# Sharing the setup of a short convolution among three engines, and reordering the mode mix behind it

## The chip, the cores and the metric

The kernel runs on one core of a Trainium2 chip. The core has a matrix engine (TensorE, PE in the rows), a vector engine (VectorE, DVE), an activation engine (ScalarE, ACT), GpSimd (POOL), and SyncE (SP). POOL issues all loads here, because they cast from float32 to bfloat16 on the way, and SP issues all stores. The metric is the time of one execution on the device, in microseconds (us).

## The reference

The input x has 8 batches of 3264 rows of 192 channels. First each row becomes a weighted sum of itself and the six rows ahead of it, with seven weights per group of 24 channels (8 groups). Then the 64 lowest Fourier modes along the rows are mixed by a complex 192x192 matrix each, and transformed back, and a dense layer with a relu is added.

```python
w = softmax(weight, axis=-1)                    # (8 groups, 7 taps)
x = einsum('hk,bskhg->bshg', w, windows_of_7(x)) # causal, zeros ahead of row 0
X = rfft(x, axis=1)[:, :64]
Yr = Xr @ w_r - Xi @ w_i                        # for each mode, 192x192
Yi = Xr @ w_i + Xi @ w_r
u = x + irfft(Yr + 1j * Yi, n=3264)
out = u + maximum(u @ w_ch, 0)
```

## The kernel before

The rows of a batch are cut into 27 windows of 122 rows. A window is loaded with the six rows ahead of it as 128 partitions, and all of x stays in SBUF as `x_all`. The work runs in three stages, in an order that is written out in the code: each engine works through its own queue in that order.

**Stage one: setup, convolution and Fourier transform.** The convolution of a group of channels is one matmul with a band matrix `cband[:, h, :]` (128x128, the seven taps on seven diagonals). VectorE builds the eight bands: for each tap, `copy_predicated` (L163) writes the tap's weight where the mask `maskk` of that diagonal is set, four groups at a time. VectorE also prepares the angles for the Fourier matrix `fst` (`kprod`, `turns`, L167 to L173), and ScalarE turns them into sines and cosines (`make_f`, L176 to L178). A batch is three units (10, 8 and 9 windows), 24 units in all. For a unit, `conv_unit` makes two halves of four matmuls each into one of two PSUM buffers, and ScalarE copies each half back over `x_all` (L233). `dft_unit` then multiplies the unit's windows with `fst` (L284); it follows the convolution by 5 units at the start and by 1 at the end (`lag`). After a batch's third unit VectorE copies the sums out (`xs`, L288), PE sorts them by mode (L296), and VectorE writes them to `xt` (L298).

**Stage two: the mode mix.** It has 16 groups of four modes. In each group PE multiplies `xt` with the modes' weights (`yp`, L349), ScalarE copies the product (`ymix`), PE transposes it (`et`), and VectorE writes `yeT`. Weights lie in tiles `wt` of two modes with six buffers (`MG = 2`, L205): a group's two tiles are loaded anew as soon as its matmuls are through, for use three groups later. Between these steps the 24 units of x are transposed into `cT` for the last stage (`t_unit`): VectorE first copies the upper 64 channels together (`make_tail`, L240 to L243, two buffers), PE transposes some 14 blocks into two PSUM tiles `tp` (L271), and VectorE copies each out (L273). Two units stand in each of groups 0 to 7, one in each later group. `g_part` transposes `fst` in groups 8 to 11.

**Stage three: the output.** For each pair of batches and windows PE sums the inverse transform and the dense layer in PSUM (`group_z`), ScalarE applies the relu (L409), PE adds the plain sum (`group_y`), VectorE adds x (L425), and SP stores.

```python
for _ in range(2 if g < 8 else 1):
    if tq and g < NG4 - 1:
        t_unit(*tq.pop(0))
if gq and g >= 8:
    g_part(gq.pop(0))
```

Of the kernel before, what the change touches and what calls it, by code (L numbers as in the profile page):

```python
# [9 lines left out]
ALU = mybir.AluOpType  # L10
# [8 lines left out]
def kernel(  # L19
# [24 lines left out]
    GW = NWIN * WIN + 6  # L44
    MG = 2
    NGRP = MODES // MG
# [18 lines left out]
    def load_unit(b, u):  # L65
# [10 lines left out]
        else:  # L76
# [25 lines left out]
                   allow_small_or_imprecise_dtypes=True)  # L102
    load_unit(0, 0)
    load_unit(0, 1)
    maskk = sp.tile([P, KK, P], BF16, tag="maskk")
# [6 lines left out]
    for u in range(3):  # L112
        load_unit(1, u)
    nc.gpsimd.memset(ident[:], 0.0)
    nc.gpsimd.affine_select(out=ident[:], in_=ident[:], compare_op=ALU.not_equal, fill=1.0,
                            base=0, pattern=[[-1, P]], channel_multiplier=1)

# [5 lines left out]
    for b in range(2, B):  # L123
        for u in range(3):
# [9 lines left out]
                            in1=midx[:, :].unsqueeze(1).to_broadcast([P, NWIN, MODES]),  # L134
                            op=ALU.mult)
    wmax = sp.tile([P, H], F32, tag="wmax")
    nc.vector.reduce_max(out=wmax[:], in_=wraw[:], axis=AX.X)
# [4 lines left out]
    nc.scalar.activation(out=wexp[:], in_=wsub[:], func=ACT.Exp)  # L142
    nc.vector.memset(cband[:], 0.0)
    wsum = sp.tile([P, H], F32, tag="wsum")
# [9 lines left out]


    wps = pxx.tile([P, 512], F32, tag="xp", name="wps")
    wsb = wps[:, 0:H * KK].rearrange("p (h k) -> p h k", h=H)
    nc.vector.tensor_tensor(out=wsb, in0=wexp[:],
                            in1=wrec[:, :].unsqueeze(2).to_broadcast([P, H, KK]), op=ALU.mult)
    for half in range(2):  # L160
        hs = slice(4 * half, 4 * half + 4)
        for k in range(KK):
            nc.vector.copy_predicated(  # L163
                out=cband[:, hs, :],
                mask=maskk[:, k, :].bitcast(mybir.dt.uint16).unsqueeze(1).to_broadcast([P, 4, P]),
                data=wsb[:, hs, k:k + 1].to_broadcast([P, 4, P]))
    nc.vector.tensor_scalar(out=turns[:], in0=kprod[:], scalar1=1.0 / S, scalar2=MAGIC,  # L167
                            op0=ALU.mult, op1=ALU.add)
    nc.vector.tensor_scalar(out=turns[:], in0=turns[:], scalar1=-MAGIC, scalar2=float(S),
                            op0=ALU.add, op1=ALU.mult)  # L170
    nc.vector.tensor_tensor(out=kprod[:], in0=kprod[:], in1=turns[:], op=ALU.subtract)
    nc.vector.tensor_scalar(out=kprod[:], in0=kprod[:], scalar1=-float(S) / 2, scalar2=float(S) / 2,
                            op0=ALU.max, op1=ALU.min)  # L173

    def make_f():
        nc.scalar.activation(out=turns[:], in_=kprod[:], func=ACT.Abs)  # L176
        nc.scalar.activation(out=fst[:, :, 1:2 * MODES:2], in_=kprod[:], func=ACT.Sin, scale=-TWOPI / S)
        nc.scalar.activation(out=fst[:, :, 0:2 * MODES:2], in_=turns[:], func=ACT.Sin, scale=-TWOPI / S,  # L178
                             bias=halfpi[:, 0:1])
# [24 lines left out]

    wp = early_stack.enter_context(tc.tile_pool(name="wts", bufs=6, side="right"))  # L205
    wtiles = {}
# [7 lines left out]

    for g in range(6):
        load_weights(g)
    workp = early_stack.enter_context(tc.tile_pool(name="work", bufs=2, side="right"))

    def conv_unit(b, u):
        w0, n = UNITS[u]  # L220
        if u == 0 and b > 0:
            nc.vector.memset(x_all[0:OV, b, 0, :], 0.0)
        for half in range(2):
# [8 lines left out]
            srcv = cp[0:WIN, :, 0:GRP * n].rearrange("p j (w e) -> p j w e", w=n)  # L232
            nc.scalar.copy(out=dst, in_=srcv)  # L233

# [28 lines left out]

    def t_unit(b, u):
        s0, n = USLOTS[u]
        h1 = (n + 1) // 2
        tl = make_tail(b, u)
# [37 lines left out]
    for i, (b, u) in enumerate(units):  # L305
        conv_unit(b, u)
        if i == 3:
            make_f()
            setup_stack.close()
# [30 lines left out]
    NG4 = MODES // 4  # L340
    tq = [(b, u) for b in range(B) for u in range(3)]
    gq = list(range((NWIN + 7) // 8))
    for g in range(NG4):
        yp = pconv.tile([P, 512], F32, tag="cv", name="yp")
        for j in range(3):
            for pos in range(4):
# [4 lines left out]
                                 start=(j == 0), stop=(j == 2), tile_position=(0, 32 * pos))  # L351
        for i in range(4 // MG):
            n = 6 + (4 // MG) * g + i
            if n < NGRP:
                load_weights(n)
# [12 lines left out]
        if g == NG4 - 2:  # L368
            while tq:
                t_unit(*tq.pop(0))  # L370
    early_stack.close()
# [132 lines left out]
```

## Time and profile before

| what | value |
|---|---|
| median of 3 runs | 230.06 us (228.36 to 232.61) |
| profiled execution, its own time | 230.81 us |
| span of its instructions | 229.1 us |
| PE busy | 167.1 us, 73% |
| DVE busy | 116.4 us, 51% |
| ACT busy | 101.4 us, 44% |
| POOL busy | 70.6 us, 31% |
| read from and written to HBM | 40.31 MB and 20.05 MB |

Busy times are sums over the whole span. The three stages have different limits, so a stage is read by itself: what it waits for, and what ends that wait. A row of the kind "start, length, engine, line" is one instruction or several merged ones, and the bracket at its end says how long the engine had been idle and who released it.

### The profile page before, as it was taken

What the parts mean: (1) busy time and instruction counts of PE and PEld (TensorE: products, weight loads), DVE (VectorE), ACT (ScalarE), POOL (GpSimd) and SP (SyncE); (2) the same over time, 40 slices, a digit from 0 to 9 for tenths busy, and PEclk for the clock granted to TensorE, in tenths of its full rate; (3) what the DMA queues carried; (4) which work ended last, traced back from release to release, by engine and by line L of the source; (5) the groups of instructions that cost most, each with busy time, mean ns of one, the idle gap of its engine ahead of it and who ended that gap; (6) DMA issues with size and microseconds to landing.
All of it is one profiled execution on the core that took longest, in us unless ns stands there. A gap on an engine that the chain in (4) does not pass through costs nothing.

```text
span 229.1 us, 4342 instructions
## 1 busy us (share of the span) xinstructions
PE 167.1 (73%) x1699; PEld 131.8 (58%) x1699; DVE 116.4 (51%) x211; ACT 101.4 (44%) x132; POOL 70.6 (31%) x121
## 2 busy tenths in 40 slices
PE   0037349989988786768869679999899899989300
PEld 0014248777877564547647458778677677767200
DVE  7897001111111577776654615677676566666510
ACT  2017978778687010100431126566556456546200
POOL 8996343443290457574856000000000000000000
PEclk9999999999999689997995979999999999999965
DMA  2999999999998389999999401899899789988992
GB/s 28 180 177 192 192 192 192 192 192 193 184 140 142 54 129 141 156 163 140 145 183 159 83 1 38 232 245 253 217 269 254 214 207 263 249 250 241 263 263 61
DMA packets 65340, 40.50 MB, mean 177 GB/s; under 512 B 31016, under 2 KB 65320, under 8 KB 65320
## 3 DMA queue, kind: packets, MB, share of 16 engines
q0 software_dynamic: 37600, 20.14, 67.4%
q1 hardware_dynamic: 27720, 20.09, 31.8%
q8 instruction: 13, 0.21, 0.4%
q14 instruction: 7, 0.06, 0.1%
HBM read 40.31 MB, written 20.05 MB: 263 GB/s over the span
## 4 chain that ended last, share of the span: by engine, by line
DMA 33%; PE 31%; DVE 14%; POOL 8%; issue 3%; ACT 3%; SPq 3%; DVEq 0%; POOLq 0%; ACTq 0%
DMA x_all<-in_x_dram 16%; DMA out_dram<-t 8%; DVE cT L273 6%; PE tp L271 6%; DMA wt<-in_moe_w_i_dram 6%; DVE t L425 5%; PE zp L400 5%; PE zp L407 5%; PE zp L405 5%; POOL x_all L63 5%; PE zp L414 4%; DMA win<-in_moe_w_ch_dram 4%; SPq L431 3%; ACT x_all L233 2%; PE yp L349 2%
## 5 line engine op out<-in xcount | busy, mean ns | idle before, releaser
L425 DVE TENSOR_TENSOR t<-zp,x_all 122x768 f32<-122x768 f32 (+1 forms) x54 | 51.3, 957 | 32.3 <-PE zp L414 21.7
L409 ACT ACTIVATE zp<-zp 128x768 f32<-128x768 f32 x54 | 42.9, 795 | 31.4 <-PE zp L407 31.4
L233 ACT CAST x_all<-cp 122x960 bf16<-122x960 f32 (+2 forms) x48 | 39.5, 884 | 22.5 <-PE cp L227 22.3
L405 PE MATMUL zp<-win,cT 128*128 128x192 bf16 x216 | 45.2, 249 | 0.0
L227 PE MATMUL cp<-x_all,cband 128*128 128x240 bf16 (+2 forms) x192 | 27.7, 286 | 19.7 <-DVE cband L163 15.2
L400 PE MATMUL zp<-zwi,gst 128*128 128x384 bf16 x108 | 35.9, 332 | 5.4 <-DVE t L425 4.0
L273 DVE COPY cT<-tp 128x854 bf16<-128x854 bf16 (+2 forms) x48 | 26.9, 590 | 18.3 <-PE tp L271 17.8
L227 PEld LDWEIGHTS <-cband 128*128 128x128 bf16 x192 | 19.4, 108 | 25.2 <-DVE cband L163 15.6
L63 POOL DMA_DIRECT2D x_all<-in_x_dram x24 | 23.8, 1001 | 15.9 <-DMA x_all<-in_x_dram 15.9
L271 PE MATMUL tp<-ident,tl 122*128 122x122 bf16 x112 | 23.2, 243 | 7.0 <-DVE tl L240 5.4
L211 POOL DMA_DIRECT2D wt<-in_moe_w_r_dram x32 | 19.3, 602 | 28.3 <-PE yp L349 21.7
L271 PE MATMUL tp<-ident,x_all 122*128 122x122 bf16 x216 | 26.4, 242 | 2.1 <-DVE cT L273 1.9
L284 PE MATMUL xp<-x_all,fst 122*128 122x192 bf16 (+1 forms) x216 | 22.3, 252 | 7.4 <-ACT fst L178 6.2
L405 PEld LDWEIGHTS <-cT 128*128 128x128 bf16 x216 | 21.4, 99 | 10.5 <-issue 7.7
L414 PE MATMUL zp<-zwi,gst 128*128 128x384 bf16 x108 | 26.2, 326 | 0.2 <-ACT zp L409 0.2
L407 PEld LDWEIGHTS <-cT 128*128 128x128 bf16 x216 | 21.4, 99 | 7.4 <-issue 0.5
L357 ACT CAST ymix<-yp 128x192 bf16<-128x192 f32 x16 | 5.1, 319 | 44.2 <-PE yp L349 44.2
L284 PEld LDWEIGHTS <-fst 122*128 122x128 bf16 (+1 forms) x216 | 18.4, 100 | 8.8 <-ACT fst L178 6.6
L407 PE MATMUL zp<-win,cT 128*128 128x192 bf16 x112 | 23.3, 248 | 0.0
L271 PEld LDWEIGHTS <-x_all 122*128 122x128 bf16 x216 | 18.9, 110 | 5.7 <-issue 4.8
L407 PE MATMUL zp<-wB,cT 128*128 128x192 bf16 x104 | 21.9, 251 | 0.0
L288 DVE CAST xs<-xp 128x192 bf16<-128x192 f32 x8 | 2.9, 358 | 34.3 <-PE xp L284 34.3
(76 smaller groups left out, 158.9 us busy)
## 6 DMA issues: line engine op xcount, KB each, us to landing
out_dram<-t SPq DMA_DIRECT2D x48, 336.0 KB
wt<-in_moe_w_r_dram POOLq DMA_DIRECT2D x32, 144.0 KB, 5.1
wt<-in_moe_w_i_dram POOLq DMA_DIRECT2D x32, 144.0 KB, 5.1
x_all<-in_x_dram POOLq DMA_DIRECT2D x8, 432.0 KB, 16.1
x_all<-in_x_dram POOLq DMA_DIRECT2D x9, 384.0 KB, 17.7
x_all<-in_x_dram POOLq DMA_DIRECT2D x7, 480.0 KB, 18.4
out_dram<-t SPq DMA_DIRECT2D x48, 30.0 KB
out_dram<-t SPq DMA_DIRECT2D x8, 168.0 KB
```

The lines of the kernel that those rows point to most:

```text
L63: nc.gpsimd.dma_start(out=x_all[:, b, c0:c0 + n, :], in_=src)
L227: nc.tensor.matmul(cp[:, j, 0:GRP * n].rearrange("p (w e) -> p w e", w=n), cband[:, h, :], x_all[:, b, w0:w0 + n, GRP * h:GRP * h + GRP], ...
L233: nc.scalar.copy(out=dst, in_=srcv)
L271: nc.tensor.transpose(tp[:, WIN * k:WIN * k + WIN], slot_lhsT(b, u, tl, a + k), ident[0:WIN, 0:WIN])
L273: nc.vector.tensor_copy(out=cT[:, b, WIN * a:WIN * (a + cnt)], in_=tp[:, 0:WIN * cnt])
L284: nc.tensor.matmul(xp[:, 0:D], fst[0:k, c, :], x_all[0:k, b, c, :], start=(c == 0), stop=(c == NWIN - 1))
L400: nc.tensor.matmul(zp[:, k, 0:2 * D], gst[:, WIN * w:WIN * w + P], zwi[:, 2 * q:2 * q + 2, 0, :], start=True, stop=False, skip_group_check ...
L405: nc.tensor.matmul(o, cT[:, b, WIN * sa:WIN * sa + P], win0[:, 0:D], start=False, stop=False, skip_group_check=True)
L407: nc.tensor.matmul(o, cT[:, b, WIN * sb:WIN * sb + P], wBs[par], start=False, stop=(i == 1), skip_group_check=True)
L409: nc.scalar.activation(out=zp[:, :, 0:2 * D], in_=zp[:, :, 0:2 * D], func=ACT.Relu)
L414: nc.tensor.matmul(zp[:, k, 0:2 * D], gst[:, WIN * w:WIN * w + P], zwi[:, 2 * q:2 * q + 2, 1, :], start=False, stop=True, skip_group_check ...
L425: nc.vector.tensor_tensor(out=tv, in0=yv, in1=xv, op=ALU.add)
```

## The change

- **Band.** VectorE builds the bands of groups 0 to 3 alone (7 predicated copies instead of 14). For groups 4 to 7 ScalarE multiplies each mask with the weight of one group and tap (28 instructions, into `scaled`), PE sums the seven taps by seven matmuls with the identity into a PSUM tile `bps`, and VectorE copies that to `cband`. The identity is therefore made ahead of the second load of x on POOL.
- **Order of the setup.** The two steps that round the angles (`turns`) move ahead of the softmax. The absolute value moves from ScalarE to VectorE (a bitwise and), the clamp goes away, with a factor in the scale of the sine in its place, and `make_f` comes after the third unit instead of the fourth.
- **Copies of the convolution.** The second half of a unit is copied by VectorE in units 0 to 7 and in odd units after; ScalarE copies the rest.
- **Weights.** Tiles of four modes with three buffers instead of two modes with six: the same room and the same lead of three groups, half as many loads.
- **Mode mix.** Groups take two and one unit in turn; a unit's tail is copied ahead of the transposes of the unit before it; `g_part` comes in groups 1, 3, 5 and 7.

```diff
-    MG = 2
+    MG = 4
...
     load_unit(0, 0)
+    nc.gpsimd.memset(ident[:], 0.0)
+    nc.gpsimd.affine_select(out=ident[:], in_=ident[:], compare_op=ALU.not_equal, fill=1.0,
+                            base=0, pattern=[[-1, P]], channel_multiplier=1)
     load_unit(0, 1)
...
     wps = pxx.tile([P, 512], F32, tag="xp", name="wps")
...
+    nc.vector.tensor_tensor(out=wsb[:], in0=wexp[:], in1=wrb, op=ALU.mult)
+    nc.vector.tensor_tensor(out=wpv, in0=wexp[:], in1=wrb, op=ALU.mult)
+    scaled = sp.tile([P, KK, 4, P], BF16, tag="scaled")
+    bps = pxx.tile([P, 512], F32, tag="xt", name="bps")
+    for k in range(KK):
+        nc.vector.copy_predicated(
+            out=cband[:, 0:4, :],
+            mask=maskk[:, k, :].bitcast(mybir.dt.uint16).unsqueeze(1).to_broadcast([P, 4, P]),
+            data=wpv[:, 0:4, k:k + 1].to_broadcast([P, 4, P]))
+        for j in range(4):
+            nc.scalar.activation(out=scaled[:, k, j, :], in_=maskk[:, k, :], func=ACT.Copy,
+                                 scale=wsb[:, 4 + j, k:k + 1])
+        nc.tensor.matmul(bps[:], ident[:], scaled[:, k, :, :].rearrange("p j n -> p (j n)"),
+                         start=(k == 0), stop=(k == KK - 1))
     nc.vector.tensor_tensor(out=kprod[:], in0=kprod[:], in1=turns[:], op=ALU.subtract)
-    nc.vector.tensor_scalar(out=kprod[:], in0=kprod[:], scalar1=-float(S) / 2, scalar2=float(S) / 2,
-                            op0=ALU.max, op1=ALU.min)
+    nc.vector.tensor_copy(out=cband[:, 4:8, :].rearrange("p j n -> p (j n)"), in_=bps[:])
+    nc.vector.tensor_scalar(out=turns[:].bitcast(mybir.dt.int32), in0=kprod[:].bitcast(mybir.dt.int32),
+                            scalar1=0x7fffffff, scalar2=None, op0=ALU.bitwise_and)
...
-        nc.scalar.activation(out=turns[:], in_=kprod[:], func=ACT.Abs)
...
-    wp = early_stack.enter_context(tc.tile_pool(name="wts", bufs=6, side="right"))
+    wp = early_stack.enter_context(tc.tile_pool(name="wts", bufs=3, side="right"))
...
-            nc.scalar.copy(out=dst, in_=srcv)
+            if half == 0 or (i >= 8 and i % 2 == 0):
+                nc.scalar.copy(out=dst, in_=srcv)
+            else:
+                nc.vector.tensor_copy(out=dst, in_=srcv)
...
-        if i == 3:
+        if i == 2:
             make_f()
...
+    def t_next():
+        i = tpos[0]
+        if i == len(tunits):
+            return
+        tpos[0] += 1
+        if i + 1 < len(tunits):
+            tails.append(make_tail(*tunits[i + 1]))
+        t_unit(*tunits[i], tails[i])
...
-        for _ in range(2 if g < 8 else 1):
-            if tq and g < NG4 - 1:
-                t_unit(*tq.pop(0))
-        if gq and g >= 8:
+        for _ in range(2 - g % 2):
+            if g < NG4 - 1:
+                t_next()
+        if gq and g % 2 == 1:
             g_part(gq.pop(0))
```

ScalarE's queue, from the softmax to the first copies after the sines. Before (L233 is a convolution copy, L176 to L178 make `fst`):

```order
L142 ACT_TABLE_LOAD
L142 ACTIVATE wexp<-wsub 128x56
L233 CAST x_all<-cp 122x4x10x24 x2
L233 CAST x_all<-cp 122x4x8x24 x2
L233 CAST x_all<-cp 122x4x9x24 x2
L233 CAST x_all<-cp 122x4x10x24 x2
L176 ACTIVATE turns<-kprod 128x1728
L177 ACT_TABLE_LOAD
L177 ACTIVATE fst<-kprod 128x1728
L178 ACTIVATE fst<-turns,halfpi 128x1728
L233 CAST x_all<-cp 122x4x8x24 x2
```

The same place in the changed kernel (L244 is a convolution copy, L187 and L188 make `fst`):

```order
L146 ACT_TABLE_LOAD
L146 ACTIVATE wexp<-wsub 128x56
L175 ACTIVATE scaled<-maskk,wsb 128x128 x28
L244 CAST x_all<-cp 122x4x10x24
L244 CAST x_all<-cp 122x4x8x24
L244 CAST x_all<-cp 122x4x9x24
L187 ACT_TABLE_LOAD
L187 ACTIVATE fst<-kprod 128x1728
L188 ACTIVATE fst<-turns,halfpi 128x1728
L244 CAST x_all<-cp 122x4x10x24
```

Five of the eight copies ahead of the sines and the absolute value are gone from ScalarE, and 28 scaled masks stand ahead of the first copy.

VectorE's queue in the setup, from the rounding of the angles to the first step of the convolution. Before:

```order
L158 TENSOR_TENSOR wps<-wexp,wrec 128x56
L163 COPY_PREDICATED cband<-maskk,wps 128x512 x14
L167 TENSOR_SCALAR turns<-kprod 128x1728
L169 TENSOR_SCALAR turns<-turns 128x1728
L171 TENSOR_TENSOR kprod<-kprod,turns 128x1728
L172 TENSOR_SCALAR kprod<-kprod 128x1728
```

In the changed kernel, from the same product of `wexp` and `wrec` on:

```order
L165 TENSOR_TENSOR wsb<-wexp,wrec 128x56
L166 TENSOR_TENSOR wps<-wexp,wrec 128x56
L170 COPY_PREDICATED cband<-maskk,wps 128x512 x7
L179 TENSOR_TENSOR kprod<-kprod,turns 128x1728
L180 CAST cband<-bps 128x512
L181 TENSOR_SCALAR turns<-kprod 128x1728
```

The two roundings (now L136 and L138) have left this place for one ahead of the softmax, and the copy of the second half of the bands stands behind the subtraction.

VectorE's queue in the mode mix, over one two-unit group (tl is a tail, cT the copies out of the transposes, yeT the end of a group). Before:

```order
L366 COPY yeT<-et 128x2x64
L240 COPY tl<-x_all 122x640
L273 COPY cT<-tp 128x976
L273 COPY cT<-tp 128x854
L240 COPY tl<-x_all 122x512
L273 COPY cT<-tp 128x732 x2
L366 COPY yeT<-et 128x2x64
```

In the changed kernel, over a one-unit and a two-unit group:

```order
L388 COPY yeT<-et 128x2x64
L253 COPY tl<-x_all 122x640
L285 COPY cT<-tp 128x854 x2
L388 COPY yeT<-et 128x2x64
L253 COPY tl<-x_all 122x512
L285 COPY cT<-tp 128x976
L285 COPY cT<-tp 128x854
L255 COPY tl<-x_all 122x512
L256 COPY tl<-x_all 122x128
L285 COPY cT<-tp 128x732 x2
L388 COPY yeT<-et 128x2x64
```

The tail that is copied ahead of a unit's `cT` is now that of the next unit: the 640 wide one belongs to the unit with the 976 wide copy.

## Rows read from the trace of the kernel before

**Rows 1.** Four stretches: length; busy PE, PEld, DVE, ACT, POOL; PE clock; DMA; GB/s.

```profile
31.60:75.90 44.30, 39.28 (x416) 34.03 (x416) 7.85 (x23) 32.44 (x41) 17.48 (x29) 1.00 1.36 172
75.90:108.40 32.50, 24.57 (x332) 18.94 (x332) 22.22 (x59) 2.54 (x8) 18.68 (x32) 0.85 0.93 136
108.40:131.80 23.40, 18.01 (x249) 13.60 (x247) 13.39 (x38) 5.65 (x12) 11.72 (x20) 0.85 0.95 142
131.80:229.10 97.30, 76.78 (x664) 59.95 (x664) 53.49 (x58) 45.25 (x58) 0.00 (x0) 0.93 0.75 207
```

**Rows 2.** VectorE in order of time, setup: start, length, line.

```profile
5.68 10.40 DVE L163 CAST_PREDICATED cband<-maskk,wps 128x512 bf16<-128x512 uint16 x14
16.00 1.05 DVE L167 TENSOR_SCALAR turns<-kprod 128x1728 f32<-128x1728 f32 x1
17.09 1.30 DVE L169 TENSOR_SCALAR turns<-turns 128x1728 f32<-128x1728 f32 x1
18.43 1.96 DVE L171 TENSOR_TENSOR kprod<-kprod,turns 128x1728 f32<-128x1728 f32 x1
```

**Rows 3.** PE in order of time: convolution with the upper bands, first transform.

```profile
16.14 1.62 PE L227 MATMUL cp<-x_all,cband 128*128 128x240 bf16 x8 [3.97 <-DVE cband L163]
...
31.68 1.78 PE L284 MATMUL xp<-x_all,fst 122*128 122x192 bf16 x10 [6.22 <-ACT fst L178]
```

**Rows 4.** ScalarE in order of time, from the absolute value to the cosines.

```profile
24.50 1.66 ACT L176 ACTIVATE turns<-kprod 128x1728 f32<-128x1728 f32 x1
26.17 1.28 ACT L177 ACT_TABLE_LOAD   x1
27.46 2.11 ACT L177 ACTIVATE fst<-kprod 128x1728 bf16<-128x1728 f32 x1
29.45 2.18 ACT L178 ACTIVATE fst<-turns,halfpi 128x1728 bf16<-128x1728 f32 x1
```

**Rows 5.** Groups of ScalarE by shape: count, busy us, mean ns of one.

```profile
L392 ACT ACTIVATE zwi<-zwps,ascale 128x384 bf16<-128x384 f32 x4 | 2.3, 580 | 5.9 <-DVE zwi L390 5.9
...
L142 ACT ACTIVATE wexp<-wsub 128x56 f32<-128x56 f32 x1 | 0.2, 250 | 2.2 <-DVE wsub L139 2.2
```

**Rows 6.** The page's costliest groups: VectorE reading PSUM, ScalarE copying.

```profile
L425 DVE TENSOR_TENSOR t<-zp,x_all 122x768 f32<-122x768 f32 (+1 forms) x54 | 51.3, 957 | 32.3 <-PE zp L414 21.7
...
L233 ACT CAST x_all<-cp 122x960 bf16<-122x960 f32 (+2 forms) x48 | 39.5, 884 | 22.5 <-PE cp L227 22.3
```

**Rows 7.** Waits of PE, 31.6 to 76 us: total, times, longest.

```profile
PE cp L227 <- ACT x_all L233: 1.2, 4, 0.4
...
PE xp L284 <- ACT x_all L233: 0.7, 1, 0.7
```

**Rows 8.** Waits of PE, 76 to 131 us.

```profile
PE tp L271 <- DVE tl L240: 5.4, 11, 0.7
PE yp L349 <- DMA wt<-in_moe_w_i_dram: 2.2, 3, 1.1
```

**Rows 9.** PE in order of time: mixes of groups 0, 8, 11 and 15.

```profile
75.90 0.74 PE L349 MATMUL yp<-wt,xt 128*32 128x192 bf16 x12 [0.66 <-DVE cT L328]
...
108.41 0.54 PE L349 MATMUL yp<-wt,xt 128*32 128x192 bf16 x12
...
116.11 0.78 PE L349 MATMUL yp<-wt,xt 128*32 128x192 bf16 x12
...
130.26 0.50 PE L349 MATMUL yp<-wt,xt 128*32 128x192 bf16 x10 [0.27 <-DMA wt<-in_moe_w_i_dram]
```

**Rows 10.** The page: transfer rate in 40 slices, and the weight loads.

```profile
GB/s 28 180 177 192 192 192 192 192 192 193 184 140 142 54 129 141 156 163 140 145 183 159 83 1 38 232 245 253 217 269 254 214 207 263 249 250 241 263 263 61
...
wt<-in_moe_w_r_dram POOLq DMA_DIRECT2D x32, 144.0 KB, 5.1
```

**Rows 11.** POOL's load issues: shortest, median, longest ns; the last wait for x.

```profile
L63 POOL DMA_DIRECT2D x_all<-in_x_dram x24: 873/967/1644, 2.7 to 45.1; - x24
...
63.04 0.58 POOL L211 DMA_DIRECT2D wt<-in_moe_w_r_dram  x1 [1.45 <-DMA x_all<-in_x_dram]
```

More of the change, by code (lines that the diff above doesn't have):

```diff
@@ L113 @@
         load_unit(1, u)
-    nc.gpsimd.memset(ident[:], 0.0)
-    nc.gpsimd.affine_select(out=ident[:], in_=ident[:], compare_op=ALU.not_equal, fill=1.0,
-                            base=0, pattern=[[-1, P]], channel_multiplier=1)
     nc.gpsimd.memset(sel[:], 0.0)
@@ L135 @@
                             op=ALU.mult)
+    nc.vector.tensor_scalar(out=turns[:], in0=kprod[:], scalar1=1.0 / S, scalar2=MAGIC,
+                            op0=ALU.mult, op1=ALU.add)
+    nc.vector.tensor_scalar(out=turns[:], in0=turns[:], scalar1=-MAGIC, scalar2=float(S),
+                            op0=ALU.add, op1=ALU.mult)
     wmax = sp.tile([P, H], F32, tag="wmax")
@@ L142 @@
     nc.scalar.activation(out=wexp[:], in_=wsub[:], func=ACT.Exp)
-    nc.vector.memset(cband[:], 0.0)
+    nc.vector.memset(cband[:, 0:4, :], 0.0)
     wsum = sp.tile([P, H], F32, tag="wsum")
@@ L156 @@
     wps = pxx.tile([P, 512], F32, tag="xp", name="wps")
[L157 to L170, printed above, removed]
+    wpv = wps[:, 0:H * KK].rearrange("p (h k) -> p h k", h=H)
+    wrb = wrec[:, :].unsqueeze(2).to_broadcast([P, H, KK])
+    wsb = sp.tile([P, H, KK], F32, tag="wsb")
+    nc.vector.tensor_tensor(out=wsb[:], in0=wexp[:], in1=wrb, op=ALU.mult)
@@ L175, in make_f @@
     def make_f():
-        nc.scalar.activation(out=turns[:], in_=kprod[:], func=ACT.Abs)
-        nc.scalar.activation(out=fst[:, :, 1:2 * MODES:2], in_=kprod[:], func=ACT.Sin, scale=-TWOPI / S)
-        nc.scalar.activation(out=fst[:, :, 0:2 * MODES:2], in_=turns[:], func=ACT.Sin, scale=-TWOPI / S,
+        wfac = -TWOPI * (1.0 - 4e-7) / S
+        nc.scalar.activation(out=fst[:, :, 1:2 * MODES:2], in_=kprod[:], func=ACT.Sin, scale=wfac)
+        nc.scalar.activation(out=fst[:, :, 0:2 * MODES:2], in_=turns[:], func=ACT.Sin, scale=wfac,
@@ L213, in load_weights, with conv_unit @@
         wtiles[g] = wt
-    for g in range(6):
+    for g in range(3):
         load_weights(g)
     workp = early_stack.enter_context(tc.tile_pool(name="work", bufs=2, side="right"))
-    def conv_unit(b, u):
+    def conv_unit(i, b, u):
         w0, n = UNITS[u]
@@ L262, in slot_of, with t_unit @@
         return 3 * (w // 2) + w % 2, 3 * (w // 2) + 2, w % 2
-    def t_unit(b, u):
+    def t_unit(b, u, tl):
         s0, n = USLOTS[u]
         h1 = (n + 1) // 2
-        tl = make_tail(b, u)
         for a, cnt in ((s0, h1), (s0 + h1, n - h1)):
@@ L305 @@
     for i, (b, u) in enumerate(units):
-        conv_unit(b, u)
-        if i == 3:
+        conv_unit(i, b, u)
+        if i == 2:
             make_f()
@@ L340 @@
     NG4 = MODES // 4
-    tq = [(b, u) for b in range(B) for u in range(3)]
+    tunits = [(b, u) for b in range(B) for u in range(3)]
+    tails = [make_tail(*tunits[0])]
+    tpos = [0]
+    def t_next():
[6 more added lines that the diff above has]
+        t_unit(*tunits[i], tails[i])
     gq = list(range((NWIN + 7) // 8))
@@ L351 @@
                                  start=(j == 0), stop=(j == 2), tile_position=(0, 32 * pos))
[L352 to L355, printed above, removed]
+        if g + 3 < NGRP:
+            load_weights(g + 3)
         ymix = workp.tile([P, D], BF16, tag="ymix")
         nc.scalar.copy(out=ymix[:], in_=yp[:, 0:D])
-        for _ in range(2 if g < 8 else 1):
-            if tq and g < NG4 - 1:
-                t_unit(*tq.pop(0))
-        if gq and g >= 8:
+        for _ in range(2 - g % 2):
+            if g < NG4 - 1:
+                t_next()
+        if gq and g % 2 == 1:
             g_part(gq.pop(0))
@@ L368 @@
         if g == NG4 - 2:
-            while tq:
-                t_unit(*tq.pop(0))
+            while tpos[0] < len(tunits):
+                t_next()
     early_stack.close()
```

## The prediction

> **What bounds the kernel now.** I read the stretches first [rows 1], then the waits of PE and the order of time at the seams. The reader should see three stages with three limits.
>
> From 31.6 to 75.9 us PE works through convolutions and transforms, 39.3 us busy of 44.3: PE is the bound, with 5.0 us of gaps. It can't begin earlier than the Fourier matrix, whose cosines end at 31.6 [rows 4]; PE had idled 6.2 us for that [rows 3]. The loads are not the bound here: POOL's last wait for x ends at 63.04 [rows 11], some 13 us before the stage ends.
>
> From 75.9 to 131.8 (55.9 us) no engine is full. Groups 0 to 7 take (108.41 - 75.90) / 8 = 4.06 us each, with 22.2 us of VectorE in 32.5. PE waits there for tails that VectorE copies only after the unit before [rows 8]; the rate of transfers sinks to 129 to 163 GB/s, where it stood at 192 during the loads of x [rows 10]. From group 8 on a group holds one unit. The first three of these take (116.11 - 108.41) / 3 = 2.57 us; group 15 then ends a wait for weights at 130.26, so the last seven steps took 3.12 us on average [rows 9]. So the first half is held by the exchange of PE and VectorE while transfers idle, the second by transfers while the engines idle.
>
> From 131.8 on (97.3 us) the change touches nothing.
>
> **Stage one, part by part.** *The two roundings* move ahead of the softmax: 1.05 + 1.30 = 2.35 us [rows 2]. Everything behind them slips by that: the predicated copies, which began at 5.68, begin at 8.1, and with a second small product at 8.3. Seven of them take half of 10.40, so the lower bands are ready at 13.5. The subtraction (1.96) then ends at 15.4.
>
> *The scaled masks.* No row shows 128 columns on ScalarE with a scale from a tile. An activation of 56 columns takes 0.25 us, one of 384 columns with such a scale 0.58 [rows 5]; on the line between them 128 columns take 0.32. Back to back I take 0.30, so 28 take 8.4 us. The bounds are 7.0 us, by the 0.25 of the smaller row, and 10.6 us, by 0.38, which is 0.58 less 256 columns at 0.8 ns; that slope is an estimate from 0.88 us for 864 columns on average and 0.25 for 56 [rows 5, 6]. They start at 8.0 and end at 16.4. The Trainium skill ("ScalarE: Activation LUTs", What ACT_TABLE_LOAD costs) adds some 93 ns to an activation per pointer operand and lets neighbours overlap by as much; by its figures 28 would take an estimated 8.2 us, and the sum would not move by more than 0.2 us.
>
> *What follows.* PE's queue has the seven identity matmuls ahead of the first convolution, so even the lower half waits: first convolution at 16.8, upper bands copied at 17.5 (0.7 us for 512 columns out of PSUM, from 957 ns for 768 [rows 6]). The upper half of the convolution started at 16.14 [rows 3], so the band is **later**, by 1.4 us, not earlier. VectorE does the bitwise and (1.05 as L167; up to 1.96 if it runs at the pace of the subtraction), then the second halves at 1.2 us per 960 columns (957 ns for 768, scaled). Stepping through two PSUM buffers: unit 0 copied by 19.8, unit 1 by 21.3, ScalarE's third copy ends at 21.7. Then table load, sines and cosines, 1.28 + 2.11 + 2.18 = 5.6 us with the absolute value's 1.66 gone [rows 4]: `fst` at 27.3 instead of 31.6. Unit 3 still waits for a copy, so unit 4 is convolved by 29.3. Before, units 0 to 4 were through when the transform began at 31.68. **Gain 2.4 us** (0.5 to 4).
>
> *Copies on two engines.* Of PE's 5.0 us of gaps, 1.2 + 0.7 us are waits for ScalarE's copies [rows 7]; two engines copying in parallel should take most of these: **gain 1.5 us** (0 to 3). VectorE has 7.85 us to do in 44.3 [rows 1], so 16 more copies of some 1.1 us (17.6 us) fit. That cover is what makes them free. The mix then starts at 72.0 instead of 75.9.
>
> *POOL.* The identity now delays the second load by two small steps. The longest of POOL's 24 issues of x took 1644 ns against a median of 967 [rows 11]; it ran beside the roundings, which so cost an issue up to 0.7 us. In their new place they run beside the first loads. I charge nothing, because the stage ends 13 us after the last wait for x; without that cover it costs 1 to 2 us. The Trainium skill ("SBUF — State Buffer", Who interferes with whom) says more: a VectorE step of this kind can lock GpSimd out until it ends, and the descriptors of loads wait so long. By that rule x would come up to an estimated 2.4 us later, still under the same cover; the longest issue agrees with a part of such a lock.
>
> **Stage two, part by part.** *Tails ahead.* The waits for tails are 5.4 us in 11 records [rows 8], 0.49 us each. Without them a two-unit group takes 4.06 - 0.98 = 3.08 us and a one-unit group 2.57 - 0.49 = 2.08 (a `g_part` in it, which four of the eight have). Sum: 8 x 3.08 + 8 x 2.08 = 41.3 us. VectorE's own work, 22.2 + 13.4 = 35.6 us [rows 1], lies below.
>
> *Transfers.* Three groups of weights are there at the start, 13 follow, each four loads of 144 KB = 0.59 MB. At 192 GB/s [rows 10] that is 3.07 us, close to the 3.12 of the last seven groups. 13 x 3.1 = 40.3 us, from about 2.5 us after the first mix (matmuls, issue, first bytes). So transfers end 42.8 us after the start.
>
> *Balance.* Both limits come to some 42 us, because the units are now spread evenly; before, the halves had one limit each. From the last matmuls to the next stage are 1.5 us more (130.26 to 131.8). Floor: 44.3. Two limits of the same size hinder each other, for which I add 2 us: **46.4 instead of 55.9, gain 9.5 us** (4 to 12).
>
> *Bigger tiles* halve POOL's issues; a load of 144 KB lands after 5.1 us (median) [rows 10], and a group has three groups' time, 9 us. I charge nothing: two groups are in flight meanwhile.
>
> **Sum.** 2.4 + 1.5 + 9.5 = 13.4 us. The profiled execution's own time is 230.81 us, so 217.4. It lay 0.75 us above the median of the three runs, so on their footing 216.7.
>
> **Rivals.**
> *The tail was not the wait.* PE and VectorE hand two `tp` buffers to and fro. If the wait for the tail gives way to one for a free `tp`, groups stay at 4.06 and 2.57: 8 x 6.63 + 1.5 = 54.5 us, gain 1.4 there, 5.3 in all: about 225. For it: VectorE is busy 68% in the first half, and the buffers are the same. Against: a tail step is only 0.3 us long while PE stands for 0.49.
> *Both floors are reached*, and stage one sheds its gaps: 42.5 us for the mix, 6 us in stage one: 19.4 in all, 210.7. Against: nothing in the trace runs gap-free.
> *Slower: the reload becomes the bound.* A tile of four modes is used only when both its 288 KB halves have landed, and reloaded only when all its matmuls are done. If a landing grows with the load from 5.1 us [rows 10] to over 10, three groups' time no longer covers it, and each group takes a third of landing and issue together. From 3.75 us per group on, all 13.4 us are gone (16 x 0.85 above the 2.9 of the forecast); at 4.3 us, a landing of 12, the time is 216.7 + 16 x 1.4 = 239. For it: twice the bytes travel behind one signal. Against: a group's four small loads landed one behind the other too, within the 9 us that three groups took.
> *The setup's loss wins.* If scaled masks take 10.6 us and the band is 4 us late, stage one gains nothing; stage two still gives 9.5: 220. That is inside the range.
>
> **How the numbers follow.** Forecast (213 to 222) 0.62, both floors 0.14, the tail was not the wait 0.16, reload as the bound 0.04, nothing moves for a reason unseen 0.04. The range leaves out half of the floors' case and the last two: 211 to 225. A measurement here tells about 2% from no change, below 225.5 counts as faster: 0.62 + 0.14 + 0.13 = 0.89; same 0.07; slower 0.04.
>
> **What would show it.** The first transform near 29 us, the first mix near 72, groups at about 3 us in turn of long and short, transfers near 190 GB/s throughout the mix, hardly a wait of PE for a tail, and the last stage still 97 us long. I am wrong if groups still alternate at 4 and 2.6 us, if PE waits long for weights in most groups, or if the last stage changes, say by another granted clock than 0.93 [rows 1].

## The result and the profile after

The changed kernel takes 217.99 us (median of 4 runs, 216.72 to 219.15); the kernel before, timed beside it, 231.34 (228.36 to 234.95). The ratio is 0.951, with a 95% interval of 0.939 to 0.963; like those below it leaves out runs more than 1.5% above the fastest of their kernel (the others average 229.2 and 218.0 us, a gain of 11.2). The profiled execution took 217.28 us with a span of 215.5. Stage by stage, from PE's first matmul of each kind in the two traces:

| what | before | forecast | after |
|---|---|---|---|
| first transform | 31.68 | 29.3 | 29.51 |
| start of the mix | 75.90 | 72.0 | 74.41 |
| length of the mix | 55.93 | 46.4 | 45.64 |
| length of the last stage | 97.27 | 97.3 | 95.45 |

The total came out near the forecast of 216.7 us, but not all of its terms did: stage one gave 1.5 us in place of 3.9, the mix 10.3 in place of 9.5, and the untouched last stage came out 1.8 shorter. Executions of one kernel differ by up to 3.6% here (thirteen of the kernel before: 225.4 to 233.5 us), so a stage length from one trace is good to about a microsecond or two, and only waits and orders of events are read finer than that.

The stretches of the changed kernel answer to [rows 1]; the columns are the same:

```profile
29.50:74.40 44.90, 39.17 (x418) 33.88 (x416) 19.88 (x36) 22.66 (x28) 14.52 (x23) 1.00 1.42 181
74.40:120.05 45.65, 35.45 (x580) 28.98 (x580) 34.14 (x96) 8.29 (x20) 16.03 (x26) 0.96 1.02 170
120.05:215.50 95.45, 74.90 (x664) 58.95 (x664) 53.72 (x58) 45.26 (x58) 0.00 (x0) 0.93 0.77 211
```

The first row holds the surprise: ScalarE lost 10 us of work and VectorE took 12 us on, yet the stretch is 0.6 us longer, and PE's gaps grew from 5.0 to 5.7 us. In the second row PE and VectorE do the work of before in 10 us less. Not all of that is waiting: PE is busy 35.5 us with the same matmuls, where it was 42.6 (24.57 and 18.01 in [rows 1]), and the granted clock there is 0.96, where it was 0.85.

PE in order of time, around the first convolution, the first transform and the first mix; it answers to [rows 3] and [rows 9]:

```profile
16.40 2.85 PE L237 MATMUL cp<-x_all,cband 128*128 128x240 bf16 x12
20.14 1.52 PE L237 MATMUL cp<-x_all,cband 128*128 128x192 bf16 x8 [0.89 <-ACT x_all L244]
...
28.92 0.80 PE L237 MATMUL cp<-x_all,cband 128*128 128x192 bf16 x4 [0.98 <-ACT x_all L244]
29.51 0.85 PE L296 MATMUL xp<-x_all,fst 122*128 122x192 bf16 x4
...
74.41 0.53 PE L373 MATMUL yp<-wt,xt 128*32 128x192 bf16 x12 [0.66 <-DVE xt L310]
```

ScalarE in the same setup; it answers to [rows 4]:

```profile
7.69 8.28 ACT L175 ACTIVATE scaled<-maskk,wsb 128x128 bf16<-128x128 bf16 x28 [1.07 <-DVE wsb L165]
...
23.89 2.13 ACT L187 ACTIVATE fst<-kprod 128x1728 bf16<-128x1728 f32 x1
25.88 2.18 ACT L188 ACTIVATE fst<-turns,halfpi 128x1728 bf16<-128x1728 f32 x1
```

The masks took 8.28 us (8.4 forecast). The band is later than before, as forecast: the first convolution starts at 16.40 and the upper bands are copied by 17.33, where the upper half was convolved from 16.14. The cosines end at 28.06, so the transform no longer waits for them, but for the convolution of unit 4, whose release is the bracket at 28.92.

Waits of PE from the first transform to the mix (total, times, longest), which answer to [rows 7]; the first line is one of the kernel before:

```profile
PE cp L227 <- DVE x_all L222: 1.1, 2, 0.5
...
PE cp L237 <- DVE x_all L232: 2.5, 4, 0.8
PE cp L237 <- ACT x_all L244: 0.8, 3, 0.4
PE xp L296 <- DVE x_all L246: 0.5, 1, 0.5
```

L232 (L222 before) is a memset of 0.14 us that zeroes the six rows ahead of a batch. It makes the longest sum of waits, 2.5 us where it was 1.1, and for the ScalarE copies that were to be relieved PE waits only 0.8 us.

Waits of PE in the mix, which answer to [rows 8]:

```profile
PE yp L373 <- DMA wt<-in_moe_w_i_dram: 4.9, 5, 1.5
PE tp L283 <- DVE cT L285: 3.0, 9, 0.4
PE tp L348 <- DVE cT L285: 1.3, 4, 0.3
```

No wait for a tail is left. Most now are for weights. The page's transfer rate in 40 slices (5.4 us each) and its weight loads, which answer to [rows 10]:

```profile
GB/s 22 150 177 192 192 191 195 190 193 193 193 195 176 78 118 201 199 207 204 204 205 99 0 14 245 241 245 220 261 252 251 185 248 272 253 247 249 241 264 55
...
wt<-in_moe_w_r_dram POOLq DMA_DIRECT2D x16, 288.0 KB, 6.3
wt<-in_moe_w_i_dram POOLq DMA_DIRECT2D x16, 288.0 KB, 7.1
```

In the mix the rate stands at 199 to 207 GB/s; before it sank to 129 to 163. A group's 0.59 MB at 206 GB/s is 2.9 us, which is the pace of the groups while PE waits for weights (2.88 us each from 88.72 to 108.86). A load of twice the size lands after 6.3 and 7.1 us instead of 5.1: the rival in which the reload becomes the bound needed over 10.

### The profile page after: what moved, and what is told of

Same layout as the page of the kernel before. It is cut to its first block, busy times and chain, and to the rows that moved or that the text cites. A ratio compares the mean times of both kernels' runs of the same rounds, so it can differ in the third digit from the quotient of the medians.

```text
span 215.5 us, 4334 instructions
## 1 busy us (share of the span) xinstructions
PE 161.8 (75%) x1706; PEld 128.1 (59%) x1706; DVE 127.1 (59%) x222; ACT 95.6 (44%) x143; POOL 53.8 (25%) x89
## 4 chain that ended last, share of the span: by engine, by line
DMA 41%; PE 25%; SPq 12%; POOL 7%; DVE 7%; issue 3%; ACT 0%; DVEq 0%; POOLq 0%; ACTq 0%
DMA x_all<-in_x_dram 23%; SPq L453 12%; DMA wt<-in_moe_w_i_dram 10%; DMA out_dram<-t 5%; PE zp L422 4%; PE zp L429 4%; PE zp L427 4%; PE tp L283 4%; PE zp L436 4%; POOL x_all L63 3%; DVE t L447 3%; DMA wt<-in_moe_w_r_dram 3%; PE yp L373 2%; DVE cT L285 2%; POOL wt L221 1%
## 5 line engine op out<-in xcount | busy, mean ns | idle before, releaser
L431 ACT ACTIVATE zp<-zp 128x768 f32<-128x768 f32 x54 | 42.9, 795 | 29.3 <-PE zp L429 28.7
L427 PE MATMUL zp<-win,cT 128*128 128x192 bf16 x216 | 44.4, 246 | 0.0
L422 PE MATMUL zp<-zwi,gst 128*128 128x384 bf16 x108 | 35.2, 326 | 5.0 <-DVE t L447 3.6
L244 ACT CAST x_all<-cp 122x768 bf16<-122x768 f32 (+2 forms) x32 | 26.9, 878 | 23.2 <-PE cp L237 23.2
L285 DVE COPY cT<-tp 128x854 bf16<-128x854 bf16 (+2 forms) x48 | 26.3, 587 | 10.0 <-PE tp L283 9.4
L246 DVE CAST x_all<-cp 122x960 bf16<-122x960 f32 (+2 forms) x16 | 17.0, 1064 | 22.3 <-PE cp L237 21.1
L427 PEld LDWEIGHTS <-cT 128*128 128x128 bf16 x216 | 21.1, 98 | 9.6 <-issue 6.6
L436 PE MATMUL zp<-zwi,gst 128*128 128x384 bf16 x108 | 26.2, 326 | 0.2 <-ACT zp L431 0.2
L429 PEld LDWEIGHTS <-cT 128*128 128x128 bf16 x216 | 21.1, 98 | 7.0
L283 PE MATMUL tp<-ident,x_all 122*128 122x122 bf16 x216 | 22.4, 223 | 3.2 <-DVE cT L285 3.0
L429 PE MATMUL zp<-win,cT 128*128 128x192 bf16 x112 | 23.0, 246 | 0.0
L283 PEld LDWEIGHTS <-x_all 122*128 122x128 bf16 x216 | 17.3, 101 | 6.9 <-issue 4.3
L283 PE MATMUL tp<-ident,tl 122*128 122x122 bf16 x112 | 20.5, 223 | 0.0
L221 POOL DMA_DIRECT2D wt<-in_moe_w_r_dram x16 | 9.9, 618 | 32.5 <-PE yp L373 26.2
```

The costliest lines, as they stand in the source:

```text
L422: nc.tensor.matmul(zp[:, k, 0:2 * D], gst[:, WIN * w:WIN * w + P], zwi[:, 2 * q:2 * q + 2, 0, :], start=True, stop=False, skip_group_check ...
L427: nc.tensor.matmul(o, cT[:, b, WIN * sa:WIN * sa + P], win0[:, 0:D], start=False, stop=False, skip_group_check=True)
L429: nc.tensor.matmul(o, cT[:, b, WIN * sb:WIN * sb + P], wBs[par], start=False, stop=(i == 1), skip_group_check=True)
L431: nc.scalar.activation(out=zp[:, :, 0:2 * D], in_=zp[:, :, 0:2 * D], func=ACT.Relu)
L436: nc.tensor.matmul(zp[:, k, 0:2 * D], gst[:, WIN * w:WIN * w + P], zwi[:, 2 * q:2 * q + 2, 1, :], start=False, stop=True, skip_group_check ...
```

## The experiments

Ratios are to the kernel before, timed beside each experiment; the changed kernel's own is 0.951 (0.939 to 0.963).

**1. The mix alone.** The kernel before with the new order of tails, groups and `g_part`; its weights stay in tiles of two modes, and stage one is the old one. The edit is the last two pieces of the diff of the change.

> The kernel before with the new mode mix alone (tails ahead, two and one unit in turn, transposes of fst in groups 1 to 7); tiles stay at two modes and stage one is the old one. Theory: the gain is made in the mix, whose length falls from 55.9 us to 46 to 47 us, while the mix still starts at 75.9: some 10 us less, a ratio near 0.957 to the kernel before. Rival (the earlier start or the bigger tiles make the gain): the mix stays above 52 us and the ratio above 0.98.

Measured: 220.06 us, 0.964 (0.952 to 0.976), which is some 8 us. In its trace, of an execution of 221.02 us, the mix starts at 76.48 and takes 47.2 us.

**2. Stage one alone.** The changed stage one with the mix of the kernel before.

```diff
-            tails.append(make_tail(*tunits[i + 1]))
-        t_unit(*tunits[i], tails[i])
+        tl = make_tail(b, u)
...
-        for _ in range(2 - g % 2):
+        for _ in range(2 if g < 8 else 1):
...
-    MG = 4
+    MG = 2
```

> The changed setup and copies alone; mix and tiles as in the kernel before. Theory: the first transform near 29.5 us, the mix starts near 74.4 instead of 75.9 and takes 56 us as before, ratio 0.99 to 1.0. Rival (the setup is what gains): mix start below 73 or a mix below 52 us, ratio under 0.98.

Measured: 227.57 us, 1.002 (0.997 to 1.007, ten runs). Stage one by itself gives nothing that can be measured, though its trace starts the mix 0.9 us earlier (75.01). In this trace the old mix took 52.9 us at a granted clock of 0.94, where the trace before took 55.9 at 0.85. So up to 3 us of the mix's 10.3 came between two executions of the same mix. The 8 us of experiment 1 lie between the 10.3 and the 7.2 that are left.

**3. Tails late.** The changed kernel, but a unit's tail is copied at its own turn.

```diff
-        if i + 1 < len(tunits):
-            tails.append(make_tail(*tunits[i + 1]))
-        t_unit(*tunits[i], tails[i])
+        t_unit(*tunits[i], make_tail(*tunits[i]))
```

> The changed kernel, but each tail is copied right before the transposes of its own unit, as before; two and one unit still in turn. Theory of the prediction (each tail in the way costs PE 0.49 us, 24 of them 11.8 us, of which transfers at 2.9 us a group would have hidden a part): the mix takes 52 to 55 us instead of 45.6, groups alternate near 4 and 2.6 us. Rival (even spreading of units is what matters, tails wait under the transfers anyway): mix below 48 us.

Measured: 223.43 us, 0.979 (0.967 to 0.991). In its trace, of an execution of 224.36 us, the mix takes 50.5 us at a granted clock of 0.91, in place of 45.6 at 0.96; that is nearer the theory's 52 to 55 than the rival's 48, and in neither. PE's waits there, behind a line of the kernel before that goes with the 5.4 us of [rows 8]:

```profile
PE tp L271 <- DVE tl L242: 1.6, 4, 0.5
...
PE tp L283 <- DVE tl L253: 4.5, 10, 0.5
PE tp L283 <- DVE cT L285: 2.7, 8, 0.4
PE tp L283 <- DVE tl L255: 2.3, 7, 0.5
...
PE yp L370 <- DMA wt<-in_moe_w_i_dram: 0.7, 1, 0.7
```

With the tails late, 6.8 us of waits for them (L253, L255) return, about the 7.0 of the kernel before, and 4.2 of the 4.9 us for weights go. The wait for a tail was real: by the ratios (0.979 against 0.951) it is the largest single part of the gain, and taking it away uncovers the transfers.

**4. Two units first.** The changed kernel with two units in each of groups 0 to 7, one in each later group, and `g_part` from group 8 on.

```diff
-        for _ in range(2 - g % 2):
+        for _ in range(2 if g < 8 else 1):
...
-        if gq and g % 2 == 1:
+        if gq and g >= 8:
```

> The changed kernel, but two units in each of groups 0 to 7 and one in each later group, and the transposes of fst in groups 8 to 11, as before; tails stay ahead. Theory (with tails ahead a two-unit group takes 3.1 us, close to the 2.9 us in which transfers bring a group, so either order keeps the transfers busy): mix 45 to 48 us, within 2 us of the changed kernel. Rival (spreading is what matters): mix 50 us or more, first half near 4 us a group.

Measured: 219.84 us, 0.962 (0.949 to 0.976); mix 46.6 us, of which 5.7 us are waits for weights. The even spread is worth 0.9 us in the traces, no more than executions differ by.

**5. Tiles of two modes** (`MG = 2`, six buffers, two loads of each tensor per group) in the changed kernel.

> The changed kernel with tiles of two modes and six buffers as before; the rest changed. Theory (the same bytes travel with the same lead, so size costs and gives nothing): mix 45.6 to 47.5 us, within 1 us of the changed kernel's execution. Rival (a transfer of 288 KB uses the queue better, 206 GB/s against 192 to 200, or halving the issues matters): mix 48 us or more.

Measured: 220.27 us, 0.965 (0.958 to 0.972). The mix takes 47.5 us at a granted clock of 0.93, and POOL is busy 30.4 us of it in place of 16. Experiment 6 has the mix of the changed kernel word for word and took 47.3 us at 0.89, so the 1.9 us can't be put down to the tiles, and the intervals of the ratios overlap. Open.

This kernel differs from that of experiment 2 by the order of the mix alone, and from the changed one by the tiles alone. The mix of experiment 2, and this one:

```profile
75.00:127.90 52.90, 38.91 (x580) 29.52 (x580) 34.93 (x96) 8.29 (x20) 30.46 (x52) 0.94 0.97 147
...
74.40:121.90 47.50, 38.26 (x579) 30.62 (x579) 34.77 (x97) 8.39 (x20) 30.42 (x52) 0.93 1.01 164
```

PE is busy 38.9 and 38.3 us at like clocks; the order alone takes 5.4 us out of the stage, most of it out of PE's gaps.

**6. All convolution copies on ScalarE.**

```diff
-            if half == 0 or (i >= 8 and i % 2 == 0):
-                nc.scalar.copy(out=dst, in_=srcv)
-            else:
-                nc.vector.tensor_copy(out=dst, in_=srcv)
+            nc.scalar.copy(out=dst, in_=srcv)
```

> The changed kernel with all copies of the convolution on ScalarE. Theory of the prediction (two engines in parallel take 1.5 us of PE's waits away): the mix starts 1 to 2 us later than the 74.4 us of the changed kernel. Rival from the trace (what ScalarE's copies cost less, VectorE's queue gives back, since the zeroing of the next batch's first rows stands behind a copy there: 2.5 us of waits against 1.1): mix start within 0.7 us of 74.4, waits for the zeroing back near 1.1 us.

Measured: 220.05 us, 0.965 (0.956 to 0.973). The mix starts at 75.69, 1.3 us later than in the changed kernel. But 1.1 of that arises ahead of the first transform (30.61 against 29.51): ScalarE has three more copies ahead of its table load, which starts only 0.3 us later for it, but units 3 and 4 wait for their turn behind the cosines. After the first transform the split gains only 0.2 us, no more than traces of the same code differ by. PE's waits there:

```profile
PE cp L237 <- ACT x_all L243: 1.3, 4, 0.4
PE cp L237 <- DVE x_all L232: 1.1, 2, 0.6
PE xp L293 <- ACT x_all L243: 0.7, 1, 0.7
```

The waits for ScalarE are back at 2.0 us (from 0.8), and those for the zeroing sink from 2.5 to 1.1: VectorE's copies had put one wait in the place of the other.

**7. Roundings late.** The two steps that round the angles stand behind the predicated copies again.

```diff
-    nc.vector.tensor_scalar(out=turns[:], in0=kprod[:], scalar1=1.0 / S, scalar2=MAGIC,
-                            op0=ALU.mult, op1=ALU.add)
-    nc.vector.tensor_scalar(out=turns[:], in0=turns[:], scalar1=-MAGIC, scalar2=float(S),
-                            op0=ALU.add, op1=ALU.mult)
...
+    nc.vector.tensor_scalar(out=turns[:], in0=kprod[:], scalar1=1.0 / S, scalar2=MAGIC,
+                            op0=ALU.mult, op1=ALU.add)
+    nc.vector.tensor_scalar(out=turns[:], in0=turns[:], scalar1=-MAGIC, scalar2=float(S),
+                            op0=ALU.add, op1=ALU.mult)
     nc.vector.tensor_tensor(out=kprod[:], in0=kprod[:], in1=turns[:], op=ALU.subtract)
```

> The changed kernel with the two rounding steps behind the predicated copies, ahead of the subtraction, instead of ahead of the softmax. Theory (the roundings delay masks and loads: they ran beside the identity, which took 0.99 us instead of 0.29, and the second load, 1.48 instead of 0.94): identity near 0.3 us, first convolution near 14.1 instead of 16.4, mix start 0.5 to 1.5 us earlier. Rival (the same VectorE work in another order ends at the same time, and PE is the bound afterwards): first transform and mix start within 0.5 us of the changed kernel.

Measured: 216.10 us, 0.947 (0.939 to 0.955). First convolution 14.53, first transform 28.02, mix start 73.02: 1.4 us earlier than in the changed kernel. The ratio alone does not stand clear of 0.951, but the six traces with the changed kernel's stage one (experiments 2 to 5 and 11 beside its own) start the mix between 73.94 and 75.01. The masks start at 5.82 in place of 7.69, released by another engine, and the roundings now lie where VectorE waited 1.35 us for `bps`.

```profile
5.82 8.28 ACT L171 ACTIVATE scaled<-maskk,wsb 128x128 bf16<-128x128 bf16 x28 [1.37 <-POOL maskk L112]
```

POOL in order of time, first in the changed kernel:

```profile
4.03 0.99 POOL L105 TENSOR_SCALAR_AFFINE_SELECT ident<-ident 128x128 bf16<-128x128 bf16 x1
4.96 1.48 POOL L63 DMA_DIRECT2D x_all<-in_x_dram  x1
...
12.69 0.80 POOL L121 TENSOR_SCALAR_AFFINE_SELECT sel<-sel 128x64 bf16<-128x64 bf16 x4
```

and in this experiment:

```profile
4.02 0.30 POOL L105 TENSOR_SCALAR_AFFINE_SELECT ident<-ident 128x128 bf16<-128x128 bf16 x1
4.27 0.91 POOL L63 DMA_DIRECT2D x_all<-in_x_dram  x1
...
11.44 4.32 POOL L121 TENSOR_SCALAR_AFFINE_SELECT sel<-sel 128x64 bf16<-128x64 bf16 x4
```

The roundings run from 3.79 to 5.96 in the one, from 11.34 to 13.48 in the other, with the subtraction of 1.96 us behind them. POOL's step beside them is drawn out each time: 0.30 to 0.99 us, 0.80 to 4.32.

**8. Zeroing early.** The memset of a batch's first six rows is issued two units earlier, ahead of that unit's copies, instead of with the batch's own first unit.

```diff
-        if u == 0 and b > 0:
-            nc.vector.memset(x_all[0:OV, b, 0, :], 0.0)
+        if u == 1 and b + 1 < B:
+            nc.vector.memset(x_all[0:OV, b + 1, 0, :], 0.0)
```

> The changed kernel with the zeroing of a batch's first six rows issued two units earlier on VectorE, ahead of the copies and sums that now delay it. Theory (PE's 2.5 us of waits for the zeroing are the price of VectorE's new copies): these waits vanish, and the mix starts near 72.3 us instead of 74.4; 2 us less in all, if the mix is not then held by weights that land no earlier. Rival (PE then waits for the copies or sums in its place): mix start within 0.7 us of 74.4.

Measured: 215.59 us, 0.945 (0.940 to 0.951). The first transform stays at 29.50, the mix starts at 72.64, 1.8 us earlier:

```profile
72.64 0.53 PE L373 MATMUL yp<-wt,xt 128*32 128x192 bf16 x12 [0.66 <-DVE xt L310]
```

PE's waits from the first transform to the mix begin with

```profile
PE cp L237 <- ACT x_all L244: 0.8, 3, 0.4
PE yp L373 <- DVE xt L310: 0.7, 1, 0.7
```

and no wait for the zeroing is among them.

**9. Both (7 and 8).**

> The changed kernel with both orders at once: VectorE's rounding copies of the two identities stand behind its first work on the band, and the zeroing of x_all stands ahead of the conv copies. If the two losses lie one after the other on the way to the mix (1.4 us ahead of the first conv matmul, 1.8 us between the first transform and the mix), they add: first conv matmul near 14.5 us, first transform near 28.0, mix start near 71.2 us, mix 45.5, last stage 95, time 213.0 to 214.5 us, ratio to the kernel before 0.935 to 0.945. The rival says that another limit lies close behind: x's loads still end near 63 us, or the first weights come too late for the earlier start. By it the mix starts no earlier than 72.3 us, or the mix lengthens by what its start gains, and the time stays at 215 to 216 us.

What the expectation calls copies of the two identities are the two steps that round the angles.

Measured: 213.90 us, 0.930 (0.920 to 0.940), the fastest of the variants that compute all. First transform 28.02, mix start 70.43, mix 45.7, last stage 95.5. The two add, and 0.8 us more than that. PE in order of time behind the first transform, first in experiment 8:

```profile
32.54 1.48 PE L296 MATMUL xp<-x_all,fst 122*128 122x192 bf16 x8
33.82 1.55 PE L237 MATMUL cp<-x_all,cband 128*128 128x240 bf16 x8
```

and in this one:

```profile
31.06 1.27 PE L296 MATMUL xp<-x_all,fst 122*128 122x192 bf16 x8
32.16 0.98 PE L237 MATMUL cp<-x_all,cband 128*128 128x240 bf16 x8
```

The same matmuls take less time here: 0.21 and 0.57 us of the 0.8. Why PE comes to its short durations earlier in this trace no run shows.

**10. The whole band on VectorE.** Fourteen predicated copies as before, no scaled masks, no sum on PE; all else as changed.

```diff
-        for j in range(4):
-            nc.scalar.activation(out=scaled[:, k, j, :], in_=maskk[:, k, :], func=ACT.Copy,
-                                 scale=wsb[:, 4 + j, k:k + 1])
-        nc.tensor.matmul(bps[:], ident[:], scaled[:, k, :, :].rearrange("p j n -> p (j n)"),
-                         start=(k == 0), stop=(k == KK - 1))
...
+    for half in range(2):
+        hs = slice(4 * half, 4 * half + 4)
+        for k in range(KK):
+            nc.vector.copy_predicated(
+                out=cband[:, hs, :],
+                mask=maskk[:, k, :].bitcast(mybir.dt.uint16).unsqueeze(1).to_broadcast([P, 4, P]),
+                data=wsb[:, hs, k:k + 1].to_broadcast([P, 4, P]))
```

> The changed kernel with the whole band built by VectorE, as the kernel before builds it: 14 predicated copies a half, no scaled masks on ScalarE, no sums of them on TensorE. My sums from the rows (a predicated copy near 0.24 us, 28 in place of 14 per pair of halves) put the upper band at about 19 us in place of 16 to 17, the first transform near 30.5 us in place of 29.5 and the mix start about 1 us behind the changed kernel's 74.4; time 218.5 to 219.5 us. The rival says that the shared band gains nothing: ScalarE's 28 scaled masks (8.3 us) stand ahead of its cosines and sines, so that taking them away brings the tables earlier by as much as the band comes later. By it the first transform comes at 29.5 us or earlier, and the mix starts at 74.4 us or earlier.

Measured: 220.01 us, 0.957 (0.949 to 0.964). The lower half is convolved from 13.26 on, the upper from 18.21; the first transform comes at 31.28, the mix at 76.35. The shared band is worth 1.8 us at the first transform and 1.9 at the mix, about twice what I expected (the expectation counts the copies double; they are 14 in place of 7): the fourteen copies run to 18.15 and push the subtraction, and with it the sines, back (the cosines end at 29.84, against 28.06).

**11. Half the weights.** Groups with an odd number from 3 on use the weights of the group before them and load none, so seven groups multiply with weights that are not theirs.

```diff
-            load_weights(g + 3)
+            if (g + 3) % 2 == 0:
+                load_weights(g + 3)
+            else:
+                wtiles[g + 3] = wtiles[g + 2]
```

> The changed kernel with six of the thirteen later weight loads: the groups with an odd number from 3 on multiply with the weights of the group before them, so that seven groups use the wrong weights and half of the traffic of the mix goes away (3.5 of 7.7 MB). If the transfers hold the mix (PE's 4.9 us of waits for weights in the changed kernel), these waits go and the mix, 45.6 us long, falls to what the engines need: 41 us by the forecast's sum, so 40.5 to 42.5, and the time to 213 to 215 us. The rival says that the waits for weights only take the place of the exchange of PE and VectorE over the transposes: without them PE waits as long for cT, and the mix stays at 44.5 to 45.6 us, the time at 217 to 218.

Measured: 212.08 us, 0.930 (0.920 to 0.941). The mix takes 39.8 us, at the granted clock of the changed kernel (0.96) and 91 GB/s:

```profile
73.90:113.70 39.80, 34.96 (x579) 28.72 (x579) 34.09 (x97) 8.18 (x20) 7.38 (x12) 0.96 0.61 91
```

Its waits begin with

```profile
PE tp L283 <- DVE cT L285: 2.5, 8, 0.4
PE tp L348 <- DVE cT L285: 1.3, 4, 0.3
```

and have none for weights; those for `cT` are no longer than before. So transfers hold the changed mix, by 5.9 us over what the engines need, and the exchange of PE and VectorE doesn't take their place. The run also halves POOL's work of issuing them (7.4 us busy for 16.0); but experiment 5 doubles that, and PE's waits for weights are 4.2 us there, no longer than the 4.9 here.

## Why the prediction was right in the total, and where its terms were off

**The sum: near by luck in part.** Experiments 2 and 5 lie between the two kernels, each step a single part of the change: stage one, then the order of the mix, then the tiles. The ratios are 1.002, 0.965 and 0.951, and the mix, from the kernel before on, took 55.9, 52.9, 47.5 and 45.6 us at granted clocks of 0.85, 0.94, 0.93 and 0.96. So stage one, forecast at 3.9 us, gives nothing that the ratios show, though its traces start the mix about 1.5 us earlier. The order of the mix, forecast at 9.5, gives some 8 us by the ratios and 5.4 in the traces. The last 1.4 points, some 3 us, fall to the tiles, which the forecast put at nothing, or to the difference between executions; which of them is not shown. By the ratio the whole gain is 11.2 us where 13.4 were forecast.

**First transform: right.** 2.2 us gained of 2.4, by the steps named: masks 8.28 us, the copy of `bps` 0.69, the bitwise and 1.05, the copies 0.96 to 1.16, then unit 4 as the last thing waited for. Experiment 10 shows, in its trace, that without the shared band most of it is gone.

**Copies on two engines: the step that failed.** I had 1.5 us for waits on ScalarE and wrote that VectorE's free time is the cover that makes 16 more copies free. The waits on ScalarE did fall, from 1.9 to 0.8 us. But VectorE works through one queue in order, and the memset of 0.14 us that PE needs for a batch's next convolution now stood behind copies that were waiting for PE. PE's waits for it rose from 1.1 to 2.5 us, with some for VectorE's copies beside them, and the stretch grew by 0.6 us. Busy time was not the cover; a place in the queue was what counted. Experiment 8 shows it: with the memset moved ahead the stretch takes 43.1 us, 1.1 less than before the change, near the forecast. That holds the 1.1 us too that PE waited for the memset before; no run moves the memset without the split. Experiment 6 shows that the split's gain otherwise lies ahead of the first transform.

**Roundings and POOL: half right.** The band's slip was in the sum (its start at 8.1 forecast, 7.95 measured), and x's loads are covered as I said (the last wait ends at 63.97, before at 63.04). What I didn't ask is whether the roundings needed that place at all: experiment 7 puts them where VectorE waits anyway and starts the mix 1.4 us earlier. The cost of the early place fell on the masks and the band, not on x's loads, and by VectorE's own queue: in the changed kernel the masks wait last for `wsb`, which stands behind the roundings (bracket at 7.69), in experiment 7 for POOL's masks (bracket at 5.82). POOL's drawn-out steps lay under that wait.

```profile
63.97 0.61 POOL L221 DMA_DIRECT2D wt<-in_moe_w_r_dram  x1 [1.95 <-DMA x_all<-in_x_dram]
```

The rule that I weighed, that of the Trainium skill ("SBUF — State Buffer", Who interferes with whom), says that such VectorE steps can lock GpSimd out until they end; the drawn-out steps of experiment 7 (0.30 to 0.99 us, 0.80 to 4.32) agree with it, at both places of the roundings.

**The mix: right in the limits named, less sure in the size.** The tails went (experiment 3: 4.9 us in the traces), the rival in which `tp` takes their place is refuted (cT waits of 3.0 us after, and no tails). The engines' sum of 41.3 us was measured at 39.8 (experiment 11). The transfers' floor of 44.3 us stands against 45.6. At 199 to 207 GB/s in place of the 192 assumed they were through some 41 us after the start (the rate falls from 178 to 79 GB/s at 115.5), where 42.8 was forecast; what the engines then still had to do took 4.5 us instead of 1.5. In experiments 7 to 10 the mix ran at a granted clock of 1.00 and PE was busy 34.2 to 34.3 us instead of 35.5, yet it took 45.2 to 45.7 us, with 5.4 to 6.1 us of waits for weights: what the faster clock gave, the transfers took back. The even spread, which I made the reason why both limits come to 42 us, is not shown to matter once the tails are ahead (experiment 4). The tiles are open (experiment 5). In the rival of both floors I took 42.5 us for the mix, below its own floor of 44.3; with that it comes to 212.5 us, not 210.7.

**The last stage** is 1.8 us shorter with the same code at the same granted clock of 0.93, though I had named a change there as a sign of being wrong. In the traces of the experiments it ranges from 94.2 to 97.6 us. That and the up to 3 us that the old mix varied by were no part of the argument; they made good what stage one lacked, and that is luck. Why the granted clock of an execution stands where it does (0.85 to 1.00 in the mix over these traces) stays open.

## What to carry to other kernels

Before work is given to an engine because it has idle time, look at what small step with a waiting consumer then stands behind it in that engine's queue; here moving 0.14 us of memset was worth 1.8, and the split itself 0.2 behind the first transform. When a wait is removed, work out the next limit from rows, and test it by removing that as well: tails gave way to transfers, and halving the transfers showed 5.9 us more. Put preparations where their engine waits anyway, and not at the earliest possible place: here that gave 1.4 us.

## What the runs showed of the hardware that was not expected

- A step of GpSimd beside VectorE's roundings took 0.99 us (changed kernel) in place of 0.30 (experiment 7), and four others beside the roundings and the subtraction 4.32 (experiment 7) in place of 0.80. A load's issue behind the first took 1.48 us in place of 0.91.
- PE's matmuls after the setup ran at about half pace at first (ten transform matmuls in 1.80 us at 28.02, in 1.00 at 35.13, experiment 9), while the column of the granted clock reads 1.00 in both.
- The same mix code took 45.6 us at a granted clock of 0.96 (changed kernel) and 47.3 us at 0.89 (experiment 6), but at 1.00 no less than 45.2 (experiments 7 to 10).
- The rate of the weights' loads (199 to 207 GB/s) lies above the 192 that held during the loads of x.
